# Attention and Fourier-mixing kernel: sequence table built on VectorE from the channel table's indices, the last keys of the first group turned apart, and a new order of instructions

## The chip, the cores and the metric

The kernel runs on one core of one Trainium2 chip. The metric is the device time of one execution in microseconds. The engines have short names in the profile: PE is TensorE (PEld its weight loads), DVE VectorE, ACT ScalarE, POOL GpSimd, SP SyncE. L12 is line 12 of the kernel.

## The reference

Attention with squared relus over 8 batches, 12 heads, 448 positions and 64 dimensions per head; then a block that adds the real part of a Fourier transform over positions and channels, normalises, and applies two dense layers.

```python
scores = matmul(q, k.transpose(0, 1, 3, 2)) / sqrt(64)
attn   = matmul(maximum(scores, 0.0) ** 2 / 448, v)
x      = attn.transpose(0, 2, 1, 3).reshape(8, 448, 768)
u      = x + real(fft(fft(x, axis=1), axis=2))
un     = (u - mean(u)) / sqrt(var(u) + 1e-06)          # over the 768 channels
out    = u + maximum(un @ w_ch1, 0.0) @ w_ch2          # 768 -> 3072 -> 768
```

## The kernel before

**How the order is made.** The kernel is written as some two dozen Python generators ("streams"): loads, tables, turning of q and k, attention, mixing, dense layers, stores. Each `yield need(engine, ...)` stands for one step, and the code behind it issues the instructions of that step. `Streams.run` takes one character after another from the string `ORDER`; a character is the index of the stream whose next step comes next. Streams that are finished drop out of the numbering, and new ones are added at its end. Every engine runs its instructions in the order in which they were issued, so the string fixes each engine's order. The times in `need` and in the class are the planner's; they steer a few choices (which bank, which engine), which `CHOICES` can overrule by their running number. The first streams are 0 `loading`, 1 `build_dft`, 2 `turning`, 3 `ffns`, 4 `mixes`, 5 `first_attention`, 6 and 7 `first_channels`, 8 `attentions`, 9 `warming`.

**The head (batch 0).** GpSimd issues the loads: q, k and v of a group of four heads, the last quarter of the keys and values as two separate half loads per tensor for all three groups (`load_halves`). Meanwhile `warming` (L2202) lets TensorE multiply zeros: the first step issues two products of 512 columns, each later one a product of 252 columns (L2216); it goes on until the first channel product. VectorE builds three tables of cosines and sines for the channel transform (`build_dft`, L364): for each table a rounded product (L372), its remainder (L374) and its absolute value (L376); ScalarE takes the sines (L381), and `negative` makes a negated copy (L441). The positions' table (`seq_table`, L401, and `seq_sines`, L418) is begun on GpSimd (two iotas, a scaling, two products, L406 to L414) and ended on VectorE (L421, L423, L425) and ScalarE (L431).

q and k of a group are turned by TensorE with eight transposes each for each of two pairs of heads (`turn_on_pe`, L654, r = 0 and 1), and one copy per pair brings the result to `qkT` (L678). Batch 0 has 21 score items (seven for each group). Item i is two products (L1002), a relu on ScalarE (L1017), and a square on VectorE (L1034); the last one is squared on ScalarE (L1031). Items 0 to 2 of a group need pair 0, item 3 the last keys of both pairs, items 4 to 6 pair 1. Six blocks of values (L870, L875) follow; each block is moved out in two halves (`fold`, L719 on ScalarE or L721 on VectorE), folded on VectorE (L796), and multiplied with the channel tables (L1457). The last block is moved by ScalarE, the two before it by the engine that the planner finds sooner free, the others by VectorE. The products of the two halves of the rows leave through two copies on ScalarE and two on VectorE (L1501).

**The end of the head** (`first_tail`, L1057). Four sets of rows t = 0 to 3, each in two halves: products with the positions' table (L1079, L1082), statistics (L1102, L1109), a root on ScalarE (L1115), a scaling on VectorE (L1122), a copy of the rows (L1131), the norm (L1152 on GpSimd for t = 0, 1, 2; L1154 and L1157 for t = 3), then a turn by TensorE (L1180) and its unloading (L1196, L1200) into the input of the dense layers. Of set 1 only 63 columns are turned there; a second turn for its other 64 follows later (`turn_rows`, L1255, L1260). There are three banks of the pool BS and two of BF for all this. Before the first root, ScalarE loads the table for roots (`root_table`, L448).

**The body** begins with batch 1's first score (stream `attentions`). From there attention of batches 1 to 7 is interleaved with the dense layers (L1986, L2015, L2126, L1817), which run on as one stream on TensorE.

Of the kernel before, what the change touches and what calls it, by code (L numbers as in the profile page):

```python
# [10 lines left out]
FP32 = mybir.dt.float32  # L11
# [30 lines left out]
class Banks(Bufs):  # L42
# [30 lines left out]
CODES = '0123456789ABCDEFGHIJKLMNOPQRSTUVWXYZ'  # L73
ORDER = "".join((
    '009000000200999999999999999991111N1N029919999909199G102NN10991F111888MM4400F11L88L88884L088M84L1',
    'ML480N1LM14LL0NM040LN1LLL41O0081M14LONL4L1ON401O410LQ88LLM41Q1041MMCKKNM300KP00737KQMKKNN3LP3N0L',
    'P7O30000LQ7PLLN3N0RPJJ73JLP6LPOIIJJJJL0634ML343JLJ4LL066JKKKK666KKJJJ343I03H2229G222GHG90GGG0GGG',
    'GGGGG00GGGGGGGGGGG0GGGHGGGGGG0GGHIGGGGGGGGGHIIGGGGGGGG7GHG213GFGGGF33FFHGFGF07F17EHE0GF3E1F1FF10',
    'F0F003GE000GG3FF01H1I30E0IFE1EGGEGE3HEHH3GG1GH1I1JI303III1I1KJI189ADFFBHGF1F3HFGG3FF1031JHH1HF3J',
    'G00IGH30GG1GGF31H1IHGF31F3HFGG30F1FF31G3F1GF3GF1FF3F3133C1022212H1F0E88FGF10FGI00G1HF11HNEEI11E8',  # L80
    'JJ0L00990011IHN0IHLKG555HHIAA10IHHF1HJG1HJJ1GJGJ555GGHH100GF3II1I1H1H55EHJEHG1GG2E3GG1GEDBFBD11H',
    '1I1IH31H3JJ5555555EG5555555E0GHHGEG1I555J3100EE0HE1H3KI0001CD77E9BKKIFEEHHGIIGG1GFKI31J871J3LLIE',
    'EIFFJDJEII101NILKI33PPFIDDKOOINNK000000DNOKOFLKMEN3L3OOIGKFNDFMFLIL0MM3JMM33NNIDD000DKH7G7000KHJ',
    'GJLJJLJ3LLHJLLGFF1GHDKI3H03KFDGIIGG000GDCFCD1FG2GG32212G3KG000JJII1IJGJ1JGJ3GD1J3PJN0KGOOJNL99N1',
    '1LSJNJPDDKJJ1QPRP301RJH1QJHOOLD7JJ1HQJJGL1ONI0NGM3UOCAQTTSMSQNSMKIKMMQNRMMKPMQLMRGJM63OQHJQQPML0',
    '000KKN66LKDOH0KLONJJ367F763MMIMGIKLDD33M000D000MMIKH11KKK88KK3HNJ1CAAGHFHC1GGGIGG1FGGDF2GF32212D',
    '3JFIIHHDD1HI1JI3F1JIF1FIFK3OKINNJMM1OIIF1POJIG1OM1NGN31ABBB8KK0000000NJGIG3VNIUNUTT1WIII1XTI1VVI',
    'IU31UIIFLJ3TRSSRR1TDMPPLMDLF1URD01TTS3SSS1000D1V1VS1UPTMT31T69CHH000G3SSSJQ1Q1RDHHKJR310111RDD7G',
    'GMIII3Q000DB000QQGPIIO1EOPPGRQOGDEGENJIM6OP0OQP3PHHGQQO788KK7OOLGMON3LEK663OMOKOEMKMGELDDH33NI00',
# [134 lines left out]
def kernel(  # L224
# [139 lines left out]
    def build_dft():  # L364
# [32 lines left out]

        for m in range(3):
            yield from channel_table(m)

    def seq_table():  # L401

        f = work.tile([128, 4 * KH], FP32, name="dfty", tag="uA", bufs=1)
# [1873 lines left out]
```

## Time and profile before

| | |
|---|---|
| median of 3 runs | 564.45 us (564.25 to 564.74) |
| the profiled execution's own time | 564.12 us |
| its span in the profile | 562.1 us |
| busy share of PE, DVE, ACT, POOL | 99%, 76%, 59%, 30% |

The span is the profile's time axis; the execution's own time has some 2 us more around it. A row of the timeline gives the start, the length, the engine, the line and the operation, the tiles (written first, then read), their shapes, and behind x how many instructions are merged; in square brackets stands the idle time in front and what ended it. Fillers count as busy time.

### The profile page before, as it was taken

The page shows a single profiled execution, that of the slowest core. Times are in us where ns is not written, and L with a number is a line of the kernel's source. Part 1 is how long each engine was busy: PE and PEld are TensorE (multiplying, and loading weights), DVE is VectorE, ACT ScalarE, POOL GpSimd, SP SyncE. Part 2 cuts the span into 40 slices and gives each one's busy share as a digit, 9 for nine tenths or more (in the row PEclk, how much of TensorE's full clock was granted, in tenths as well). Part 3 has the DMA queues.
Part 4 walks back from the last instruction along what each step waited for, and adds up shares of the span by engine and source line. Part 5 has one row for each costly group of instructions (what it writes and reads, how often), then busy time and mean ns, then how long its engine had stood idle before and what let it go on. Part 6 is the DMA issues. An engine that isn't in the chain of part 4 may idle for free.

```text
span 562.1 us, 11345 instructions
## 1 busy us (share of the span) xinstructions
PE 555.1 (99%) x4306; PEld 363.7 (65%) x4306; DVE 427.1 (76%) x1035; ACT 330.2 (59%) x557; POOL 166.8 (30%) x255
## 2 busy tenths in 40 slices
PE   8999999999999999999999999999999999999997
PEld 4376456576467554556756756856768688668864
DVE  7976576889787888887898788787898648544762
ACT  5977772777769678765686776657517054015400
POOL 8966224443334514434423243111011100000000
PEclk9999999999999999999999999999999999999999
DMA  9999999999999997999799989952445502314013
GB/s 111 180 206 266 204 208 147 183 172 172 147 120 222 146 195 144 142 239 184 124 153 183 214 165 166 207 139 64 114 117 159 162 30 47 96 42 141 1 43 114
DMA packets 152692, 82.46 MB, mean 147 GB/s; under 512 B 118077, under 2 KB 147901, under 8 KB 152637
## 3 DMA queue, kind: packets, MB, share of 16 engines
q0 software_dynamic: 57056, 33.63, 42.2%
q1 hardware_dynamic: 95580, 48.09, 39.9%
q8 instruction: 34, 0.56, 0.4%
q14 instruction: 22, 0.17, 0.1%
HBM read 62.91 MB, written 26.25 MB: 159 GB/s over the span
## 4 chain that ended last, share of the span: by engine, by line
PE 95%; DVE 1%; DMA 1%; ACT 1%; issue 0%; POOL 0%; DVEq 0%; POOLq 0%
PE psF L1986 27%; PE psF L2126 22%; PE psS L1002 8%; PE psS L2126 7%; PE psS L1817 7%; PE psF L875 5%; PE psF L2015 4%; PE psS L1482 2%; PE psF L1817 2%; PE psF L2040 1%; PE psF L870 1%; DMA kn<-in_k_dram 1%; PE psS L875 1%; PE psF L671 1%; PE psS L1457 1%; PE psS L1290 1%
## 5 line engine op out<-in xcount | busy, mean ns | idle before, releaser
L1017 ACT ACTIVATE sq<-psS 128x896 bf16<-128x896 f32 x168 | 145.9, 918 | 39.5 <-PE psS L1002 39.2
L1986 PE MATMUL psF<-unT,w 128*128 128x256 bf16 (+1 forms) x1296 | 165.6, 285 | 0.0
L1986 PEld LDWEIGHTS <-w 128*128 128x128 bf16 x1296 | 124.9, 98 | 38.0 <-issue 5.8
L2126 PEld LDWEIGHTS <-hT 128*128 128x128 bf16 x720 | 69.8, 98 | 47.0 <-issue 2.1
L1034 DVE TENSOR_TENSOR sq<-sq 128x896 bf16<-128x896 bf16 x138 | 82.5, 620 | 10.5 <-ACT sq L1017 9.9
L1973 ACT ACTIVATE hT<-psF 128x512 bf16<-128x512 f32 (+3 forms) x132 | 63.6, 503 | 41.3 <-PE psF L1986 40.8
L2126 PE MATMUL psF<-w,hT 128*128 128x384 bf16 x336 | 59.4, 326 | 0.0
L1674 DVE TENSOR_TENSOR o<-psF,o 128x384 f32<-128x384 f32 x73 | 40.4, 553 | 22.2 <-PE psF L2126 16.7
L1002 PE MATMUL psS<-qkT 64*128 64x448 bf16 (+1 forms) x336 | 51.8, 355 | 1.0 <-DVE qkT L678 0.9
L1832 ACT COPY copies<-psS 128x256 f32<-128x256 f32 x51 | 17.7, 376 | 53.5 <-PE psS L1817 40.2
L1391 POOL DMA_INDIRECT ubot<-u,backs x15 | 16.0, 1064 | 75.9 <-DVE u L1327 46.7
L1002 PEld LDWEIGHTS <-qkT 64*128 64x128 bf16 (+1 forms) x336 | 12.9, 94 | 32.7 <-issue 26.9
L524 POOL DMA_DIRECT2D qn<-in_q_dram x21 | 15.4, 735 | 61.7 <-DVE qkr L631 47.2
L875 PE MATMUL psF<-sq,vn 128*64 128x448 bf16 x234 | 31.5, 363 | 0.0
L1817 PEld LDWEIGHTS <-w 128*128 128x128 bf16 x288 | 28.2, 98 | 4.4 <-issue 0.7
L1334 DVE BATCH_NORM_STATS2 stats<-u 112x6 f32<-112x384 f32 (+2 forms) x56 | 29.8, 550 | 1.5 <-POOL u L1325 1.3
L737 DVE TENSOR_SCALAR xT<-psF 128x224 bf16<-128x224 f32 x56 | 19.8, 386 | 14.4 <-PE psF L875 14.1
L1391 POOL DMA_INDIRECT nbot<-un,backs x12 | 14.3, 1190 | 52.9 <-ACT un L1353 51.7
L1353 ACT ACTIVATE un<-u,small 112x768 bf16<-112x768 f32 (+2 forms) x28 | 28.7, 1029 | 1.3 <-DVE small L1340 0.9
L524 POOL DMA_DIRECT2D kn<-in_k_dram x21 | 16.1, 768 | 44.8 <-DVE qkr L631 37.8
L499 POOL DMA_DIRECT2D kn<-in_k_dram x42 | 25.8, 623 | 9.8 <-PE psF L1986 7.9
L1031 ACT ACTIVATE sq<-sq 128x896 bf16<-128x896 bf16 x30 | 28.3, 950 | 0.4
(245 smaller groups left out, 926.1 us busy)
## 6 DMA issues: line engine op xcount, KB each, us to landing
out_dram<-o SPq DMA_DIRECT2D x55, 192.0 KB, 3.5
qn<-in_q_dram POOLq DMA_DIRECT2D x21, 224.0 KB, 5.5
vn<-in_v_dram POOLq DMA_DIRECT2D x24, 192.0 KB, 6.5
w<-in_moe_w_ch_dram POOLq DMA_DIRECT2D x12, 384.0 KB, 10.7
w<-in_moe_w_ch_dram POOLq DMA_DIRECT2D x4, 1152.0 KB, 21.2
kn<-in_k_dram POOLq DMA_DIRECT2D x21, 192.0 KB, 5.8
utop<-u SPq DMA_DIRECT2D x12, 336.0 KB, 4.2
o<-utop SPq DMA_DIRECT2D x16, 192.0 KB, 2.6
```

The source lines that it names most:

```text
L524: nc.gpsimd.dma_start(out=to, in_=src[b, hs, 0:rows].rearrange("h (p j) d -> p h (j d)", j=j))
L875: nc.tensor.matmul(av[h * Dh:(h + 1) * Dh, 0:S], lhsT=vn_home[:, at:at + Dh], rhs=sq[:, h, :], start=start, stop=stop, skip_group_check=True)
L1002: nc.tensor.matmul(sc[:, h, 0:S].rearrange("k (c q) -> k c q", c=4), lhsT=flat[ps, k0:k0 + KB], rhs=qT[ps, pair], start=True, stop=True)
L1017: nc.scalar.activation(r, sc[:, :, 0:S], AF.Relu)
L1034: nc.vector.tensor_tensor(r, r, r, op=ALU.mult)
L1334: nc.vector.bn_stats(stats[:n, hf, :], u[:n, hf * (D // 2):(hf + 1) * (D // 2)])
L1391: nc.gpsimd.indirect_dma_start(out=bot, out_offset=bass.IndirectOffsetOnAxis(ap=(back if b < PAR else back2)[ch][:n], axis=0), in_=get(us[ ...
L1674: nc.vector.tensor_tensor(o[:, cols], pc[:, cols], o[:, cols], op=ALU.add)
L1817: nc.tensor.matmul(ps[:, 0:N], lhsT=lhs, rhs=rhs[:, m], start=(start and m == 0), stop=(stop and m == 2), skip_group_check=True)
L1973: nc.scalar.activation(hs, ps, AF.Relu)
L1986: nc.tensor.matmul(ph[:, i * N:(i + 1) * N], lhsT=w1_sb[m][hf][:, (jj + i) * 128:(jj + i + 1) * 128], rhs=unT[:, m, 0:N], start=(m == 0), ...
L2126: nc.tensor.matmul(pc[:, cols], lhsT=lhs[i], rhs=rhs[i][:, cols], start=(start and i == 0), stop=(i == KP - 1), skip_group_check=True)
```

## The change

1. **Sequence table.** GpSimd's part goes. The row indices are scaled copies of the channel table's, the column indices are read from its `dcol2` (0, 1, 2, ... stored as evens and odds, so read with a stride). For each of the two halves of 240 columns VectorE makes a rounded product and its remainder, then one absolute value of 480. The table is built behind the three channel tables in `build_dft`; its sines are taken when they were.
2. **Absolute value** in the channel tables by clearing the sign bit.
3. **Loads.** The iotas are issued behind the first q load, ahead of the first k load. The value halves go ahead of v of group 1.
4. **Last keys apart.** In group 0 the two pairs are turned with three of the four key quarters; four more transposes and one copy of 256 columns bring the last quarter of both pairs. Item 3 waits for it, items 0 to 2 and 4 to 6 do not.
5. **The last square** of batch 0 goes to VectorE.
6. **`root_table`** no longer names the first copies; the third norm is made by ScalarE in two halves; set 1 is turned once with 127 columns, and its second 64 are copied out at the end (`second_part`), until when its bank is kept.
7. **A new `ORDER`** (2,930 characters instead of 2,935) and new `CHOICES`.

The head's order, read character by character from the two strings (T q, T k: transposes of a pair; F: filler steps; s: score; sq: square; v: value; the number behind is the item; b: block; n: negation; c: copy of a turned pair):

```
PE, before:  F17 | T q r0 | F10 | T k r0 | F2 | T q r1, T k r1 | F3 | s0 s1 | F6 | s2 | F3 | s3 | T q | s4 | F1 | ...
             with 20 filler steps between s1 and the last values
PE, after:   F39 | T q r0 | F8 | T k r0 (six) | T q r1, T k r1 (six) | T last keys | s0 s1 s2 s3 | T q | v b0 | s4 | ...
             with 1 filler step between s1 and the last values
DVE, before: tables 0 1, n0, table 2, n1, c r0, n2, c r1, sq 0 1 2 3, ... sq 18, fold b0, sq 19, fold b1 b2,
             round, subtract, absolute (positions), fold b3 b4 b5, copies out
DVE, after:  tables 0 1 2, c r0, round, n0, c r1, n1, c last keys, subtract, n2, round, sq 0 1 2, subtract, sq 3, ...
             sq 16, (move b3), sq 17, fold b2 (half), b0, b1, absolute, fold b2 (half), b3, (move b4),
             sq 19, sq 18, sq 20, fold b4, fold b5, copies out
ACT, before: ... relu 20, move b4, sq 20, move b5, three sines, copies out, copy of batch 1's first pair, root table,
             rows t = 0, root 0, rows, ... root 3, unload 0, norm 3, unload 2, unload 3, rows 3
ACT, after:  ... relu 20, two sines, move b5, third sine, copies out, root table, rows 0, root 0, rows 0, rows 1,
             copy of batch 1's first pair, root 1, rows 1, rows 2, root 2, rows 2, norm 2 (two halves), root 3,
             unload 0, norm 3, unload 2, unload 3, rows 3
PE, channel products, before: the last three blocks' behind five fillers, one after another
PE, channel products, after:  b0 to b3, 16 transposes of batch 1, values of items 18 19 20, rest of b3, b4, F4, b5
```

(Brackets: a step that runs on VectorE or ScalarE, as the planner's times choose.)

```diff
-CODES = '0123456789ABCDEFGHIJKLMNOPQRSTUVWXYZ'
+CODES = '0123456789ABCDEFGHIJKLMNOPQRSTUVWXY'
 ORDER = "".join((
-    '009000000200999999999999999991111N1N029919999909199G102NN10991F111888MM4400F11L88L88884L088M84L1',
...
+    '0009000002009999999999199999999991999919999991N1N999999919092119999NN99919002121G220NN2G255212N5',
...
 CHOICES = {
...
     def build_dft():
...
-            nc.vector.scalar_tensor_tensor(g, f, -1.0, f, op0=ALU.mult, op1=ALU.max)
+            nc.vector.tensor_scalar(g.bitcast(mybir.dt.int32), f.bitcast(mybir.dt.int32), 0x7FFFFFFF, None,
+                                    op0=ALU.bitwise_and)
...
+        nc.vector.tensor_scalar(row[:, 0:2], row[:, 4:6], 1.0 / S, None, op0=ALU.mult)
         nc.vector.tensor_scalar(row[:, 4:7], row[:, 4:7], 1.0 / D, None, op0=ALU.mult)
...
+        if SEQ_AT == 3:
+            yield from seq_table()
     def seq_table():
...
+        cols = dcol2.rearrange("p (t k) -> p k t", t=2)[:, 0:SX // 2]
         for i in range(2):
...
+            yield need("DVE", dve(SX))
+            nc.vector.tensor_scalar(wi, cols, drow[:, i:i + 1], None, op0=ALU.mult)
+            yield need("DVE", dve(SX))
+            nc.vector.scalar_tensor_tensor(fi, cols, drow[:, i:i + 1], wi, op0=ALU.mult, op1=ALU.subtract)
+        e = yield need("DVE", 0.4)
+        nc.vector.tensor_scalar(whole, f.bitcast(mybir.dt.int32), 0x7FFFFFFF, None, op0=ALU.bitwise_and)
+        sch.add(seq_sines(f, g, e), (0, SEQ_RANK))
...
     def root_table():
-        yield need("SP", 0.0, [dft_ready, last_relu, first_copied])
-        yield need("ACT", 1.5, [first_copied])
+        yield need("SP", 0.0, [dft_ready, last_relu])
+        yield need("ACT", 1.5, [dft_ready])
...
-            if i == 0 and x == 1:
+            if i == 0 and x == 0:
                 e = yield need("POOL", 0.55)
                 dft_indices()
...
     def loading():
-        for i in range(NG):
-            yield from load_group(i)
+        yield from load_group(0, (0, 1), (0,))
+        yield from load_halves(0, 0, NG, 1)
+        yield from load_group(0, (2,), (0,))
+        yield from load_group(1, (0, 1), (0,))
+        yield from load_halves(0, 0, NG, 2)
+        yield from load_group(1, (2,), (0,))
+        yield from load_group(2)
...
-        yield from seq_table()
...
     def turn_on_pe(b, g):
...
+        first = i == 0
+        w = 4 * R + (3 if first else 4) * KB
...
-                for c in range(4):
+                for c in range(3 if first and x else 4):
...
-            copy(pairs[:, r], pt[:, 0:4 * (KB + R)])
+            copy(pairs[:, r, 0:w], pt[:, 0:w])
...
+        if first:
+            e1 = yield need("PE", 4 * 0.07, ready[i][1:2], [BF])
...
+                    nc.tensor.transpose(pt[h * Dh:(h + 1) * Dh, r], loads[i][1][:, 3, 2 * r + h, :], ident)
+            e2 = yield need("DVE", 0.28, [e1 + LATENCY["PE"]])
+            nc.vector.tensor_copy(pairs[:, :, w:], pt)
...
-            sch.add(square(b, r, e + LATENCY["ACT"], sqs[i][1], b == 0 and i == NB - 1), (0.2, 0.2))
+            sch.add(square(b, r, e + LATENCY["ACT"], sqs[i][1]), (0.2, 0.2))
...
         def turn(t, k):
             n, idn, c0, w = turned_cols(t)
+            if t == 1:
+                idn, w = rev[:, 0:127], 127
...
         def unload(t, en, part=None):
...
-                BS.give(pts[t][0], last)
+                if t != 1:
+                    BS.give(pts[t][0], last)
...
+        def second_part():
+            e = yield need("DVE", dve(6 * 64), [done[1][0]])
+            nc.vector.tensor_copy(groups[1][2][:, :, 0:64].rearrange("p (h m) w -> p h m w", h=2),
+                                  pts[1][0][:, :, 0:384].rearrange("p h (m w) -> p h m w", w=128)[:, :, :, 63:127])
+            BS.give(pts[1][0], e)
...
-        yield from norm(2, 0, "POOL")
+        yield from norm(2, 0, "ACT")
+        yield from norm(2, 1, "ACT")
...
-        sch.add(turn_rows(uns[0][1], max(t_un[1]), 128, rev[:, 63:127], 0, 64, "DVE", second_un[0]), (1, 1))
+        sch.add(second_part(), (1, 1))
```

117 lines of the change are left out of this document (58 added, 59 removed), and 38 rows, old and new, of the table CHOICES.

## The prediction

> **What bounds the kernel now.** I read the page first (its span, and the chain of waits by engine), then busy time by stage, then the timeline of the head, and last the groups of VectorE.
>
> ```profile
> span 562.1 us, 11345 instructions
> PE 95%; DVE 1%; DMA 1%; ACT 1%; issue 0%; POOL 0%; DVEq 0%; POOLq 0%
> ```
>
> The chain that ended last is 95% TensorE, but this average mixes a head, where fillers count as work, with a body. So the stages (columns: window, length, then busy time of PE, PEld, DVE, ACT, POOL):
>
> ```profile
> 10.40:28.50 18.10, 18.02 (x162) 7.57 (x161) 17.11 (x35) 18.00 (x24) 17.25 (x50) 1.00 1.32 175
> 34.60:45.60 11.00, 10.57 (x114) 8.18 (x111) 8.61 (x26) 8.16 (x18) 7.27 (x10) 1.00 1.08 222
> 45.60:558.70 513.10, 512.45 (x3906) 338.64 (x3906) 389.67 (x941) 294.68 (x500) 129.22 (x172) 1.00 0.80 145
> ```
>
> From 45.6 us to the last product TensorE is idle for 0.65 us of 513.10, and no filler is in it. The products there are the same after the change. So the body can hardly be shortened by taking waits out of it, only lengthened, and what the change can win is the moment at which the body begins: 45.6 now. In 10.40:28.50 (batch 0's scores) TensorE, ScalarE and VectorE are all nearly full; VectorE has 0.99 us free. The head's start and end, in the timeline:
>
> ```profile
> 1.27 4.09 PE L2216 MATMUL psS<-warm 128*128 128x512 bf16 x18 [1.27 <-DVE warm L319]
> 2.18 0.82 POOL L524 DMA_DIRECT2D qk<-in_k_dram  x1
> 3.19 0.52 POOL L312 IOTA dcol<- 128x386 f32 x1
> 3.30 0.59 DVE L385 TENSOR_SCALAR drow<-drow 128x3 f32<-128x3 f32 x1 [0.98 <-POOL drow L310]
> 4.00 0.44 DVE L372 TENSOR_SCALAR dftr<-dcol,drow 128x386 int32<-128x386 f32 x1
> 5.12 0.56 DVE L376 SCALAR_TENSOR_TENSOR dfty<-dfty 128x386 f32<-128x386 f32 x1
> 5.32 0.39 PE L671 MATMUL psF<-ident,qk 112*64 112x112 bf16 x8
> 5.64 1.25 PE L2216 MATMUL psS<-warm 128*128 128x252 bf16 x10
> 7.59 0.24 PE L671 MATMUL psF<-ident,qk 128*64 128x128 bf16 x1 [0.30 <-DMA qk<-in_k_dram]
> 9.31 0.65 DVE L678 COPY qkT<-psF 128x960 bf16<-128x960 bf16 x1
> 10.43 11.83 ACT L1017 ACTIVATE sq<-psS 128x896 bf16<-128x896 f32 x14
> 27.89 0.61 DVE L1034 TENSOR_TENSOR sq<-sq 128x896 bf16<-128x896 bf16 x1
> 28.79 1.01 ACT L1031 ACTIVATE sq<-sq 128x896 bf16<-128x896 bf16 x1
> 30.75 0.38 PE L875 MATMUL psF<-sq,vn 128*64 128x448 bf16 x2
> 31.18 0.61 ACT L719 ACTIVATE xT<-psF 128x224 bf16<-128x224 f32 x2 [1.38 <-PE psF L875]
> 33.50 1.05 ACT L1501 CAST pc<-psS 128x386 bf16<-128x386 f32 x2
> 34.72 0.96 ACT L678 COPY qkT<-psF 128x960 bf16<-128x960 bf16 x1 [0.16 <-PE psF L671]
> 35.68 1.28 ACT L448 ACT_TABLE_LOAD   x1
> 37.18 0.46 ACT L1131 COPY u<-psS 128x384 f32<-128x384 f32 x1
> 42.87 0.29 ACT L1115 ACTIVATE small<-small,few 112x1 f32<-112x1 f32 x1 [0.99 <-DVE small L1109]
> 43.75 0.67 ACT L1154 ACTIVATE un<-psF,small 112x384 bf16<-112x384 f32 x1
> 44.56 0.64 ACT L1196 CAST unT<-psS 128x576 bf16<-128x576 f32 x1
> 45.10 0.41 ACT L1200 CAST unT<-psS 128x291 bf16<-128x291 f32 x1
> 45.63 0.36 PE L1002 MATMUL psS<-qkT 64*128 64x448 bf16 x2
> ```
>
> The first turned keys are copied only at 9.31, although their last transpose (7.59) is long done: VectorE is still building tables. The relus (11.83 over 14, 0.845 us each) then run unbroken. At the end the last square (28.79) lets the last values go at 30.75, and on ScalarE a copy and the table load stand between 34.72 and the first rows out, 37.18. The row of 45.63 is the body's first product.
>
> **The change, part by part.** Each engine's order is the one listed above from the new ORDER string.
>
> *Start.* The iotas go ahead of the keys' load, so the indices come 0.82 us sooner (the 2.18 row); the keys land up to 0.7 later (the iotas' time, 0.52 and a little), which TensorE's fillers hide. The tiny scaling doubles: its second costs between 0.1 and 0.59 us (the 3.30 row); I take 0.1, because the long one ran beside an iota. The tables then begin near 3.3 instead of 4.00. From 4.00 to the copy at 9.31 are three tables and two negations, so a table takes 1.6 us; with the absolute value as a bit operation 0.2 less (0.56 against the 0.41 of L425 below). Three tables end near 7.5.
>
> But the copy of the keys, next on VectorE, waits for TensorE, which now runs 48 filler products before the key transposes instead of 28. The first 18 hold it to about 5.1; later ones cost 0.108 us each (the chain's row of 31.59 below: 0.54 for five). So 22 more reach 7.5, eight transposes (0.32, from 5.32 to 5.64) and eight fillers 8.7, six transposes 8.95, and the copy starts near 9.2: 0.1 sooner than now, with 1.6 us that VectorE has gained standing idle. That this copy no longer waits for the last keys buys nothing, since they have landed by then. Were the fillers at full speed from 1.27 on, the copy would come at 7.6.
>
> The page "TensorE: Matmul & The Clock Gate" of the Trainium skill, section "What's actually happening", has the array at half its clock until one window of some 3.4 us was busy, with the window free-running. The first 18 fillers against the later ten agree with half a clock; had the gate opened 0.5 us later, the copy would come some 0.25 us later still.
>
> *VectorE through the scores.* Its groups between 9.3 and 31.5 us, a row of two moves, two pieces of the chain, and ScalarE's waits for statistics (total, times, longest):
>
> ```profile
> L1034 DVE TENSOR_TENSOR sq<-sq 128x896 bf16<-128x896 bf16 x20 | 11.9, 633 | 0.7 <-ACT sq L1017 0.6
> L678 DVE COPY qkT<-psF 128x960 bf16<-128x960 bf16 x6 | 3.9, 653 | 0.2 <-PE psF L671 0.2
> L796 DVE TENSOR_TENSOR fold<-xT 128x225 bf16<-128x225 bf16 x10 | 2.3, 287 | 0.0
> L423 DVE TENSOR_TENSOR dfty<-dfty 128x480 f32<-128x480 f32 x1 | 0.7, 659 | 0.0
> L441 DVE TENSOR_SCALAR channeg<-chan 128x386 bf16<-128x386 bf16 x2 | 0.5, 261 | 0.5 <-ACT chan L381 0.5
> L425 DVE TENSOR_SCALAR dfty<-dfty 128x480 int32<-128x480 int32 x1 | 0.4, 410 | 0.0
> L421 DVE TENSOR_SCALAR dfty<-dfty 128x480 int32<-128x480 f32 x1 | 0.4, 397 | 0.0
> 23.33 0.69 DVE L721 TENSOR_SCALAR xT<-psF 128x224 bf16<-128x224 f32 x2
> 31.59 0.54 PE psS L2216 x5
> 32.13 2.00 PE psS L1457 x24
> ACT small L1115 <- DVE small L1109: 2.6, 3, 1.0
> ```
>
> From the first copy (9.31) to the end of square 19 (28.50) VectorE now does 6 copies, 20 squares, 6 moves, one negation and two folds. The new order has in the same stretch, to the end of square 20, besides these: one square (0.6); the last keys' copy (0.25: 256 columns, between the 0.26 of L441 and the 0.65 of 960 columns) less what two shortened copies save (0.14); two negations that stood before it (0.4); the sequence table's first four operations at half length (two of 0.27, two of 0.42, together 1.4: half of L421 and L423 plus a fixed part; at the least 1.06, the bare halves, and at most 2.1, the full rows, since they read with a stride); its bit operation (0.36); and six folds at 0.2 (1.2). That is 4.05. Of the 1.4 us that VectorE idles there (0.99 in the window, and L441's wait of 0.5 ahead of it) I fill 1.1. So square 20 ends near 28.5 - 0.1 + 4.05 - 1.1 = 31.3; on ScalarE it is done at 29.80. What is late next are the last values: on TensorE they stand behind 16 transposes (0.6) and two values (0.3 each) and begin near 32.0, and the move of 31.18 comes at 32.25, 1.05 later. Had VectorE kept up, ScalarE's relus and moves would end this stage 1.65 us sooner than that.
>
> *Channel products.* Today 24 short products (0.083 each) come last and end at 34.13; in the new order only eight stand behind the last fold, and they end at 34.15: level. The copies out start on ScalarE at 34.05 instead of 33.50.
>
> *Table load and rows.* The copy of 34.72 (0.96) moves behind the first rows out, so the load begins at 35.1 and the first rows leave at 36.7, 0.5 sooner. The row products end within 0.3 us of today.
>
> *Norms.* ScalarE now has that 0.96 copy and the two halves of the third norm (0.64 each by the 43.75 row, less overlap) in this stretch, which GpSimd did; its 2.6 us of waits for statistics take them in, but not where they lie best. It is free today from 41.88 (42.87 less 0.99); the third scale is there about then, the halves end at 43.25, and the fourth root comes at 43.25 instead of 42.87, the move of 44.56 at 45.1. The second rows' bank is now kept until the second part is out, so half of the last turn waits for this move, to 45.75; the move of 45.10 comes at 46.05 and frees the bank of the body's first product at 46.45, today 45.6. The six products of the second turn that are dropped (they stood just ahead of it) are inside this difference. GpSimd's sequence operations cost nothing today, as it only feeds a queue of loads; were the body short of weights, taking them out would be a gain.
>
> Sum: 564.12 us of the profiled execution (the span 562.1 and 2.0 around it) + 0.85 = 564.97. The median of the runs, 564.45, lies 0.33 above that execution, so 565.3.
>
> **The rivals.** (a) VectorE does not end the scores: its operations overlap more than I add up, or the fillers cost less. Then the 1.65 us are had: 563.7, between 563.0 and 564.4. For it: its tables are done by 7.5. Against: the 48 fillers, and 17.11 busy of 18.10.
>
> (b) Slower: blocks 3 and 4 are moved by ScalarE now, but the planner's times choose the engine, and the diff does not show which. Each on VectorE puts 0.69 us ahead of square 20. One gives 566.0, both 566.7; it decides from the second on. Against: the rule that chose ScalarE is unchanged.
>
> (c) Slower: the new order puts holes into the full body. Half of the 0.43 us that 34.60:45.60 is idle, once in each of seven batches, adds 1.5: 566.8. For it: the body has no slack to take a hole in. Against: 0.65 idle in 513.10 under the old order.
>
> (d) Slower: with the fillers gone from the scores (20 now, one then) TensorE falls back to the rate of its first products. A stretch as long as the first (4.09) adds 2 us of products where the fillers leave 2.2 free, so it decides from the second stretch on: 567.2. Against: TensorE stays busy for most of this stage without them. The same page of the Trainium skill, section "A second HAM failure mode: psum-queue depth-cycling", has frequent small pauses between groups of products bring the gate down; no run here shows that.
>
> **How the numbers follow.** Own forecast 0.50 (564.3 to 566.3), (a) 0.20, (b) 0.16, (c) 0.09, (d) 0.05. A measurement of this kernel tells about 0.2%, 1.13 us: below 563.32 or above 565.58. Of the forecast's half, 0.34 lies within and 0.16 above; (a) gives 0.10 faster and 0.10 within; (b) 0.02 within and 0.14 slower; (c) and (d) are slower. Faster 0.10, same 0.46, slower 0.44. The range takes most of (a), the price of the strided operations, and (b) and (c): 563.2 to 567.0.
>
> **What would show it.** Right: the first key copy near 9.2 with VectorE idle ahead of it; VectorE full until past 31; the last square over a microsecond behind the last relu; first rows out before 37.2; the body's first product after 46, and the body about 513 us long. Wrong: a key copy at 8 or earlier, last values before 31, or a body more than 0.5 us longer or shorter, which I hold for fixed.

## The result, and the profile after

The changed kernel took 569.75 us (median of 5 runs, 568.06 to 571.18); the kernel before, on the same chip, 564.37 (564.25 to 564.74). The ratio is 1.0092 [1.0068, 1.0116]: 0.9% slower, and above the range forecast (563.2 to 567.0). The profiled execution took 571.18, 7.06 more than that of before, and is the slowest of the five. From the page, its span and the chain of waits:

```profile
span 569.3 us, 11342 instructions
PE 89%; DVE 4%; DMA 2%; SPq 2%; ACT 2%; issue 0%; DVEq 0%
```

TensorE's share of the chain fell from 95% to 89%. The stages of after (window, length, busy time of PE, PEld, DVE, ACT, POOL, then the granted clock):

```profile
10.16:13.58 3.42, 1.84 (x28) 0.92 (x22) 3.34 (x10) 2.06 (x3) 3.27 (x8) 1.00 1.53 147
13.58:16.99 3.41, 3.41 (x28) 1.21 (x26) 2.14 (x5) 2.49 (x4) 3.35 (x18) 0.50 1.43 168
47.20:565.90 518.70, 514.18 (x3908) 339.44 (x3906) 392.30 (x942) 295.12 (x501) 131.04 (x172) 1.00 0.82 144
197.90:201.30 3.40, 2.10 (x14) 1.10 (x13) 3.37 (x8) 1.43 (x2) 1.64 (x3) 1.00 1.51 186
272.99:276.40 3.41, 1.10 (x12) 0.80 (x9) 1.60 (x4) 1.41 (x2) 0.00 (x0) 1.00 1.18 317
276.40:279.81 3.41, 3.41 (x18) 2.39 (x16) 3.38 (x8) 1.30 (x2) 0.00 (x0) 0.50 1.02 261
```

The third row is the result. The body is 518.70 us long instead of 513.10. TensorE idles 4.52 us of it instead of 0.65, so 3.87 of the 5.60 are waits. The other 1.73 are busy time for the same products: in 276.40:279.81 the granted clock is 0.50, and 3.41 us at half clock do 1.7 us of work. The half clock isn't in every execution: the run at the median, 569.75, had a mean granted clock of 1.0, and so no such window. The waits themselves, TensorE's in the body of after (what was waited for, total, times, longest):

```profile
PE psF L2021 <- DVE xT L758: 2.3, 1, 2.3
PE psF L2021 <- DMA unT<-nbot: 1.3, 1, 1.3
PE psF L2161 <- DVE o L1709: 0.4, 1, 0.4
PE psF L2021 <- DVE hT L2006: 0.3, 1, 0.3
```

Before has a single one, of 0.3, at another product (L1817). The two long ones in the timeline of after; SPq is SyncE's queue, and L1465 and L865 are DMA transposes:

```profile
195.62 1.25 SPq L1465 DMA_TRANSPOSE unT<-nbot  x1
...
201.11 1.14 PE L2021 MATMUL psF<-unT,w 128*128 128x384 bf16 x6 [1.30 <-DMA unT<-nbot]
...
266.53 3.21 SPq L865 DMA_TRANSPOSE xn<-xT  x2
...
270.36 0.76 PE L898 MATMUL psF<-sq,vn 128*64 128x448 bf16 x6
274.77 0.69 DVE L758 TENSOR_SCALAR xT<-psF 128x224 bf16<-128x224 f32 x2 [4.51 <-DMA xn<-xT]
275.51 1.93 PE L2021 MATMUL psF<-unT,w 128*128 128x256 bf16 x12 [2.31 <-DVE xT L758]
```

And the same instructions in the timeline of before:

```profile
188.37 1.23 SPq L1430 DMA_TRANSPOSE unT<-nbot  x1
...
198.29 3.09 PE L1986 MATMUL psF<-unT,w 128*128 128x384 bf16 x18
...
249.15 2.58 SPq L844 DMA_TRANSPOSE xn<-xT  x2
...
267.47 0.69 DVE L737 TENSOR_SCALAR xT<-psF 128x224 bf16<-128x224 f32 x2 [0.66 <-PE psF L875]
```

At 201 TensorE wants the turned second half of a dense input. Its transposition was issued at 195.62, 4.2 us before TensorE went idle (201.11 less 1.30 is 199.81); in before it had 9.9 us (188.37 to 198.29). At 275 VectorE may overwrite `xT` with a block of batch 5 only when batch 4's third tile has been transposed out of it. That transposition stands on SyncE behind others and was issued 3.7 us before VectorE had nothing else to do (274.77 less 4.51 is 270.26, less 266.53), 4.6 before the values to be moved were there (270.36 and 0.76); in before it was some 18 us ahead. VectorE stood 4.51 us, and TensorE behind it 2.31. So from issue to use the first transposition took 5.5 us (195.62 to 201.11) and the second 8.2 (266.53 to 274.77). For comparison the medians from issue to landing of the two kinds, of before and then of after (DMA issues: times, median us):

```profile
xn<-xT SPq DMA_TRANSPOSE x42, 5.1
unT<-nbot SPq DMA_TRANSPOSE x10, 2.7
```

```profile
xn<-xT SPq DMA_TRANSPOSE x42, 4.9
unT<-nbot SPq DMA_TRANSPOSE x10, 4.9
```

Both took longer than the median of their kind in either kernel.

The head of after, in the timeline:

```profile
1.27 7.35 PE L2251 MATMUL psS<-warm 128*128 128x512 bf16 x40 [1.27 <-DVE warm L319]
7.64 0.36 DVE L378 TENSOR_SCALAR early<-early 128x386 int32<-128x386 int32 x1
8.55 0.39 PE L680 MATMUL psF<-ident,qk 112*64 112x112 bf16 x8
10.24 0.59 DVE L687 COPY qkT<-psF 128x832 bf16<-128x832 bf16 x1 [2.23 <-PE psF L680]
15.38 0.92 ACT L1040 ACTIVATE sq<-psS 128x896 bf16<-128x896 f32 x1 [0.46 <-PE psS L1025]
29.74 0.68 ACT L740 ACTIVATE xT<-psF 128x224 bf16<-128x224 f32 x2
30.73 1.68 DVE L1057 TENSOR_TENSOR sq<-sq 128x896 bf16<-128x896 bf16 x3
32.42 0.73 PE L898 MATMUL psF<-sq,vn 128*64 128x448 bf16 x6
36.16 1.28 ACT L448 ACT_TABLE_LOAD   x1
46.27 0.64 ACT L1223 CAST unT<-psS 128x576 bf16<-128x576 f32 x1 [0.60 <-PE psS L1205]
47.27 0.37 PE L1025 MATMUL psS<-qkT 64*128 64x448 bf16 x2
```

The body begins at 47.27 instead of 45.63, 1.64 later. Of the execution's 7.06, 1.64 come from the head and some 5.5 from the body.

### The profile page after: what moved, and what is told of

It reads as the page before. It is cut to its first block, busy times and chain, and to the rows that moved or that the text cites. A ratio compares the mean times of both kernels' runs of the same rounds, so it can differ in the third digit from the quotient of the medians.

```text
span 569.3 us, 11342 instructions
## 1 busy us (share of the span) xinstructions
PE 556.5 (98%) x4295; PEld 365.1 (64%) x4295; DVE 429.2 (75%) x1040; ACT 330.9 (58%) x558; POOL 164.6 (29%) x249
## 4 chain that ended last, share of the span: by engine, by line
PE 89%; DVE 4%; DMA 2%; SPq 2%; ACT 2%; issue 0%; DVEq 0%
PE psF L2021 27%; PE psF L2161 19%; PE psS L2161 7%; PE psS L1852 7%; PE psS L1025 7%; PE psF L898 4%; PE psF L2050 4%; PE psF L1852 3%; PE psS L1517 2%; PE psS L2251 2%; DMA xn<-xT 1%; DVE sq L1057 1%; PE psF L2075 1%; PE psF L893 1%; SPq L1465 1%; DMA unT<-nbot 1%
## 5 line engine op out<-in xcount | busy, mean ns | idle before, releaser
L2021 PE MATMUL psF<-unT,w 128*128 128x256 bf16 (+1 forms) x1296 | 167.3, 286 | 3.9 <-DVE xT L758 2.3
L1426 POOL DMA_INDIRECT ubot<-u,backs x15 | 19.0, 1264 | 52.3 <-DVE u L1362 47.1
L898 PE MATMUL psF<-sq,vn 128*64 128x448 bf16 x234 | 31.3, 366 | 0.2 <-DVE sq L1057 0.2
L1426 POOL DMA_INDIRECT nbot<-un,backs x12 | 12.7, 1056 | 61.7 <-ACT un L1388 42.5
L526 POOL DMA_DIRECT2D vn<-in_v_dram x24 | 18.8, 782 | 38.9 <-PE psS L1025 38.0
L501 POOL DMA_DIRECT2D kn<-in_k_dram x42 | 25.8, 623 | 12.3 <-PE psF L2021 7.2
L1872 DVE CUSTOM_DVE_ANT_0 hT<-psS,copies 128x256 bf16<-128x256 f32 x40 | 15.9, 418 | 16.5 <-ACT copies L1867 9.6
## 6 DMA issues: line engine op xcount, KB each, us to landing
w<-in_moe_w_ch_dram POOLq DMA_DIRECT2D x12, 384.0 KB, 11.5
```

Source lines behind the costliest of these rows:

```text
L526: nc.gpsimd.dma_start(out=to, in_=src[b, hs, 0:rows].rearrange("h (p j) d -> p h (j d)", j=j))
L898: nc.tensor.matmul(av[h * Dh:(h + 1) * Dh, 0:S], lhsT=vn_home[:, at:at + Dh], rhs=sq[:, h, :], start=start, stop=stop, skip_group_check=True)
L1426: nc.gpsimd.indirect_dma_start(out=bot, out_offset=bass.IndirectOffsetOnAxis(ap=(back if b < PAR else back2)[ch][:n], axis=0), in_=get(us[ ...
L2021: nc.tensor.matmul(ph[:, i * N:(i + 1) * N], lhsT=w1_sb[m][hf][:, (jj + i) * 128:(jj + i + 1) * 128], rhs=unT[:, m, 0:N], start=(m == 0), ...
```

## The experiments

Each was timed beside the kernel before on its own chip (564.34 to 564.63). The expectations name theories by letters: A, the body's new order costs the time; B, the head does; the others stand for what is said beside them. Edits of the order are given as the engine's list, as in the change.

**Head and body apart.** The first kernel has the changed head, up to batch 1's first score, and from there the old order and choices; the second is the reverse.

```diff
-ORDER = new head + new body
+ORDER = new head + old body        # first
+ORDER = old head + new body        # second
```

> The changed kernel's head, step for step up to batch 1's first score, and behind it the steps of the body in the order and with the bank and engine choices of the kernel before. The changed kernel's profile has its body's first product at 47.27 us (45.63 before) and a body of 518.6 us (513.1 before), with TensorE waiting 2.31 us at 275.5 and 1.30 at 201.1. Theory A (the holes belong to the new body's order: its transposes by DMA and its dense products stand too close): the body is 513 us again, no wait of TensorE over 0.5 us in it, total 564.4 + 1.6 = 566.0 (565.5 to 566.5), runs within 0.5 us of one another. Theory B (the holes come from the head: it ends later, so loads and transposes are shifted against the products whatever the order): the body keeps holes of 3 to 5 us and the total stays between 568 and 571.

> The reverse: the head of the kernel before, step for step up to batch 1's first score, and the body's steps in the changed kernel's order with its choices. Theory A (order of the body): first product of the body at 45.6 as before, a body of 516 to 519 us, total 567 to 570, with a spread over the runs of more than 1 us. Theory B (late head): no holes over 0.5 us, total 564.4 plus or minus 0.5.

The new head alone: 565.77 us (565.24 to 566.74, 10 runs), 1.0022 [1.0013, 1.0031]. The new body alone: 570.23 (568.07 to 574.86, 6 runs), 1.0109 [1.0077, 1.0141], with waits of 2.5 and 1.4 us at the two places shown above. With the old body under the new head, the stage row is

```profile
47.20:560.60 513.40, 512.40 (x3907) 338.80 (x3906) 389.85 (x943) 294.66 (x500) 129.37 (x172) 1.00 0.81 145
```

513.40 us, 0.30 over before. Theory A holds, B falls: the body's order costs about 4 us behind the new head (569.75 less 565.77) and 5.7 behind the old one (570.23 less 564.51), the head about 1.3. Taken alone, body and head cost together 7.0, more than the whole change (5.4).

**Which transpositions.** Both late ones are put earlier on SyncE in the changed kernel; then only the one of batch 4.

```diff
 SyncE, batch 4:  ... nbot, q/k, xn second tile
+                 xn third and fourth tile
                  q/k, ntop, ntop, out, nbot, out
-                 xn third and fourth tile
 SyncE, batch 3:  ntop
-                 xn third tile              # only in the first of the two
                  nbot
+                 xn third tile              # only in the first of the two
```

> The changed kernel, with SyncE's queue mended at the two places where TensorE stood in its profile. The transposition of batch 4's third channel tile (and the fourth) is issued ahead of the stores and of the dense input's transpositions that stood before it (in the kernel before, too, it comes ahead of them), and at batch 3 the first transposition of a channel tile goes behind the dense input's second half instead of ahead of it. Nothing else is moved. Theory A1 (these two issues make the holes): the 2.31 us at 275.5 and the stretch of clock 0.50 behind it go, the 1.30 at 201.1 shrinks to 0.3 or less; body 513.5 to 515, total 565.8 to 567. Rival (the holes come from the crowded DMA rings or from VectorE's order, and move on): total 568 or more, with other waits of TensorE over 1 us.

> As the run before, with the first place alone (batch 4's third and fourth channel tiles). Theory A1: the wait of 2.31 us goes and the one of 1.30 stays; the total is about 1 to 1.5 us above that run's, 567 to 568.5. Rival: no gain against the changed kernel, 569 or more.

Both mended: 567.01 (564.18 to 569.4, 6 runs), 1.0053 [1.0039, 1.0067], an interval below that of the whole change. One mended: 566.19 (565.29 to 571.77, 12 runs), 1.0037 [1.0019, 1.0055]: no different from both. In the profiled execution of the first (564.18 us) TensorE's waits in the body are

```profile
PE psF L2257 <- DVE o L1805: 0.4, 1, 0.4
PE psF L2117 <- DVE hT L2102: 0.3, 1, 0.3
```

and its stages

```profile
44.90:558.90 514.00, 512.77 (x3908) 338.81 (x3906) 393.05 (x943) 295.22 (x501) 131.76 (x172) 1.00 0.81 146
10.16:13.58 3.42, 2.16 (x22) 0.90 (x19) 3.42 (x10) 3.18 (x4) 3.24 (x8) 1.00 1.60 155
```

The distances are 5.7 us at the first place (192.18 to 197.84) and some 20 at the second: no wait, no half clock, a body of 514.00. The edit moves these issues and nothing else, so these waits came from the distance between issue and use. At the second place no profile of a kernel with the mend has a wait of TensorE. But the profiled execution is the fastest of the six; the median stays some 2.5 us above before, and the runs differ by 5 us: something else is left. And since one mend does as well as two, what the place at 201 costs the median isn't shown. The kernel with one mend showed in a profiled execution of 571.25 us a wait of 1.1 at 201, which it leaves unmended, and one of 2.2 us near 103, for an addition of VectorE to the dense layers' output `o`, that the changed kernel's own trace doesn't have.

**Where in the body.** New head; the new order up to batch 3 (about 149 us) and the old one behind; the reverse; and a later cut.

```diff
-ORDER = new head + new body
+ORDER = new head + new body to 149 us + old body           # first
+ORDER = new head + old body to 149 us + new body           # second
+ORDER = new head + new body to batch 5 + old body          # third
```

> The changed kernel with its own head and its own order up to batch 3's first score (about 149 us), and from there the old order with its choices. Theory H (the loss lies where transpositions are issued close to their use, at 201 and 275): both places have the old distances, no wait of TensorE over 0.6 us behind 150; total 565.5 to 567 (the head's 1 to 2 us, and now and then a wait near 100). Rival (the loss is spread, or lies in the first 100 us of the body): 567.5 or more.

> The reverse: the changed kernel's head, the old order up to batch 3's first score, the new order behind it. Theory H: the waits near 201 and 275 are back, total 568 to 571, spread over 2 us. Rival: under 567.

> As the first of these, cut at batch 5's first score (about 245 us), so that the place near 201 is in and the one near 275 is not. Theory H: a wait of 0.5 to 2 us near 201 in most executions, none near 275; total 566.5 to 568.5, between the other two. Rival (the wait near 275 is a late consequence of the first): 565.5 to 566.5 or as much as the second.

First: 565.62 (563.95 to 569.28, 14 runs), 1.0015 [1.0007, 1.0024], level with the new head on the old body. Second: 569.89 (568.54 to 570.03, 5 runs), 1.0091 [1.0077, 1.0104], the whole loss of the change. Third: 571.53 (570.97 to 572.1, 4 runs), 1.0129 [1.0114, 1.0143]; its cut came at about 296 us, behind the last moves of batch 5, and not near 245 as its text has it, so it holds both places, and its wait of 1.4 at 276 says nothing against the theory. The second kernel's waits:

```profile
PE psF L2117 <- DVE xT L854: 2.6, 1, 2.6
PE psF L989 <- DMA vn<-in_v_dram: 1.5, 1, 1.5
PE psF L2117 <- DMA unT<-nbot: 1.3, 1, 1.3
```

The one for `vn`, batch 1's values, lies at 54 in the old order; the other two are at the known places, and this execution (570.03 us) has no half clock in its body. Waits alone can make the loss.

The first kernel's profiled execution was its slowest (569.28), with one wait, near 103, and a half clock at 104.3:

```profile
PE psF L2146 <- DVE o L1805: 3.0, 1, 3.0
```

So from batch 3 on the loss is steady, and ahead of it there is a place near 102 that costs 3 to 4 us in some executions, in this kernel too few to move the median.

**The old order with late transposes.** The same two tiles late in the kernel before:

```diff
 SyncE, batch 4:  ... xn second tile
-                 xn third and fourth tile
                  ntop, q/k, q/k, out
+                 xn third and fourth tile
```

> The kernel before, untouched but for one thing: on SyncE's queue the transpositions of batch 4's third and fourth channel tiles are issued behind the output store that follows them much later, so at about 265 instead of 249.2 and 250.5. The move into the same tile for batch 5 comes at 267.5 there. In the changed kernel the distance is 3.8 us (266.5 against 270.3) and TensorE stands for 2.3 us. Theory A1 (this distance alone makes the hole): VectorE waits 1 to 5 us for the transposition at 267.5, TensorE 0.5 to 3.5 us behind it, perhaps with a stretch of clock 0.50 after it; total 565.2 to 568.5. Rival (the hole needs the rest of the new order): total 564.2 to 564.8.

564.41 (564.23 to 565.86, 11 runs), 1.0000 [0.9990, 1.0009]. The test was weaker than meant: SyncE was free, so they were issued at 257.7, still some 10 us ahead of the move. The first of the two landed 7.4 us behind its issue. So some 10 us are enough there, and 3.7 would not have been; what that would have cost was not measured.

**VectorE slowed by GpSimd.** In the trace of after one addition takes 2.64 us where its like take 0.55, just while GpSimd does two additions (VectorE, then GpSimd):

```profile
179.97 0.55 DVE L1360 TENSOR_TENSOR u<-qs,xn 112x385 f32<-112x385 f32 x1
180.44 2.64 DVE L1362 TENSOR_TENSOR u<-tp,xn 112x383 f32<-112x383 f32 x1
...
180.92 0.93 POOL L1360 TENSOR_TENSOR u<-tp,xn 112x385 f32<-112x385 f32 x1
181.80 0.85 POOL L1362 TENSOR_TENSOR u<-qs,xn 112x383 f32<-112x383 f32 x1
```

The page "SBUF — State Buffer" of the Trainium skill, section "🔬 SBUF: two separate sides", has VectorE's operations with two inputs in SBUF and GpSimd's share a port pair that only one holds at a time, for a whole instruction. The 2.64 against 0.55 agrees: VectorE's addition ends at 183.08, behind both of GpSimd's. That it waited although it began 0.48 us before the first of them is left unexplained.

Is this the cause of the lateness? Theory G: yes. Three kernels do these additions on VectorE: one with all the mends of the last experiment below (two transpositions, fillers, iotas); the changed kernel without a mend; and one with the two transpositions mended.

```diff
-            eng, en, d = ((nc.vector, "DVE", 2 * dve(KN)), (nc.gpsimd, "POOL", 1.8))[i and not (b > 2)]
+            eng, en, d = nc.vector, "DVE", 2 * dve(KN)
```

> All mends of the run before (head with 17 first fillers, fillers in the scores, iotas behind k; both transpositions mended), and the additions of the second half of the rows of batches 1 and 2 on VectorE instead of GpSimd, at the same places of the order. Theory G (VectorE's additions are held up by GpSimd's, and what stands behind them on VectorE lets TensorE wait at about 101 and 201 us): no addition of VectorE over 0.8 us, no wait of TensorE over 0.6 us after 60 us, every execution between 563.9 and 565.2, median 564.0 to 564.6. Rival (the late loads behind these places are the cause, and VectorE gets 4.4 us more work): executions above 567 as before, or a median of 565 or more.

> The changed kernel, with the additions of batches 1 and 2 on VectorE as its only difference. Theory G: the wait of 1.30 us at 201.1 goes, the wait of 2.31 at 275.5 (batch 4's transposition) and the slow stretch behind it stay: total 566.5 to 569, 1 to 3 us under the changed kernel. Rival: no change, 569 to 571.

> The changed kernel with its own head, the body mended in all three ways (both transpositions, additions on VectorE). If the body's loss is the three places, the body is 511.5 to 513 us long and what is left is the head: two groups of executions, near 564.2 where the clock opens at about 4.5 us and near 566 where it opens at 6.5 or later and falls back in the scores; median 565 to 566. If something else in the new body costs time, 566.5 or more.

568.84 (565.7 to 571.66, 6 runs), 1.0057 [1.0036, 1.0078]; 572.33 (567.93 to 576.76, 6 runs), 1.0157 [1.0117, 1.0197]; 569.62 (566.4 to 573.94, 6 runs), 1.0095 [1.0062, 1.0129]. No addition took over 0.56 us any more. Yet the first is 4.0 us over its like without the edit (564.84, last experiment), with intervals apart, and the third 2.6 over the two mends, with intervals that just overlap. Of the second's six runs three took 567.9 to 570.0, like the whole change, and three 574.7 to 576.8. The first one's waits:

```profile
PE psF L2116 <- DMA unT<-nbot: 3.2, 1, 3.2
PE psF L2145 <- DVE o L1804: 2.1, 1, 2.1
```

The place at 201 and the one near 102 wait without a stretched addition too, so G is not shown. Nor is it ruled out for the changed kernel: the edit gives VectorE GpSimd's additions to do, where in after it is busy already for 22.26 of the 24 us from 180 on. The first wait above fits the distances again: in spite of the mend the transposition was issued at 196.93, 4.3 us before TensorE went idle (201.26), and TensorE went on at 204.49, 7.6 behind the issue.

**The head's fillers.** All with the old body: 15 fillers between the first scores; 17 first fillers instead of 39; the latter with batch 1's values loaded ahead of the second half of a weight; both kinds of filler edit, with and without that load.

```diff
 PE:  F39 | T q r0 | ... | s0 s1
+     F6
      s2
+     F3                        # and ahead of the next two scores
-PE:  F39 | T q r0
+PE:  F17 | T q r0              # few first fillers
 GpSimd, loads:
-     w1 second half, values of batch 1
+     values of batch 1, w1 second half
```

> As e1, with 15 more filler steps between batch 0's scores: six ahead of the third score, three each ahead of the fourth, fifth and sixth. In the changed kernel TensorE is busy for 1.84 of 3.42 us from 10.16 to 13.58, and the granted clock is 0.50 from 13.58 to 16.99; VectorE then waits 1.53 us for transposes at 17.25. Theory C (the missing fillers cost the clock, and the slow stretch delays the stage): no stretch of clock 0.5 behind the start, no wait of VectorE over 0.5 us between 10.3 and 32, the last square ends 1 to 1.5 us earlier than in e1 and the body begins 1 to 1.5 us earlier; total 564.5 to 565. Rival (the slow stretch lies beside ScalarE's and VectorE's own work, and fillers only take TensorE's time): body's first product within 0.3 us of e1's, total within 0.3 of e1.

> As e1, with 17 filler steps ahead of the first transposes instead of 39, as many as the kernel before has. In the changed kernel VectorE's tables end at 8.0 and the first turned keys are copied at 10.24, VectorE idle for 2.23 us ahead of it, waiting for TensorE. Theory D (the fillers hold the key transposes up): the copy starts at 8.1 to 8.8, the last square ends 1 to 2 us earlier than in e1, and the body begins 1 us or more earlier; total 564.5 to 565.2. Rival (the transposes wait for the keys' landing, or the fewer products open the clock later): copy after 9.5, body's first product within 0.4 of e1's, total within 0.4 of e1.

> The new head with 17 first fillers and the old order of the body, as in the run with fewer first fillers, and batch 1's values loaded ahead of the second half of the first dense weights instead of behind it. In that run the body began at 44.77, 0.86 us before that of the kernel before, but TensorE then waited 1.45 us at 54.40 for those values, and the median came to 565.64. Theory E (the head's gain is given back at batch 1's values, which lie behind six loads of weights): no wait for values, the last products start at about 44.8 + 511.2 = 556.0 (556.6 in the kernel before), total 563.5 to 564.2. Rival (the loads only change places and the weights come late instead, or TensorE's next wait takes over): total 565 or more.

> As the run before, with 15 filler steps more between batch 0's scores, as in the run that kept the clock up there. With fewer first fillers some executions have shown a mean clock of 0.990 to 0.997. Theory C2 (these come from slow stretches in the scores, which the fillers prevent): every execution at 0.999 or above, a smaller spread, median 0.1 to 0.4 us lower. Rival (the scores wait for loads and for ScalarE there, and fillers only delay them): median equal or up to 1 us higher.

> The new head with 17 first fillers and 15 fillers between the scores, the loads in the changed kernel's order, and the old body: the base of the next run. With the old body, batch 1's eighth relu (the row that I compare) starts at 60.62 in the kernel before and at 61.89 to 62.85 with the new head, whether the body's first product stands at 44.77 or at 47.83, and from there on the distance to the kernel before does not change any more. Theory F (the loads of batch 1 set this row, not the head's end): 61.5 to 62.5 again, median 565.3 to 565.9, no execution with a mean clock below 0.998. Rival (the head's end sets it): about 60 and 564.0.

In this order: 565.70 (564.9 to 566.73, 11), 565.64 (564.98 to 566.23, 11), 566.13 (564.93 to 568.22, 9), 565.82 (565.59 to 567.48, 7) and 566.28 us (565.58 to 567.28, 8); ratios 1.0020 [1.0012, 1.0029], 1.0019 [1.0010, 1.0028], 1.0032 [1.0020, 1.0044], 1.0027 [1.0016, 1.0038], 1.0031 [1.0020, 1.0042]. All are level with the new head unedited, and the gains expected were missed. The profiled executions (us; the clock is full from the trace's first record of a granted clock of 1.0):

| kernel | clock full from | first key copy | last square ends | body begins | last product |
|---|---|---|---|---|---|
| before | 4.92 | 9.31 | 29.80 | 45.63 | 558.49 |
| after | 6.75 | 10.24 | 32.41 | 47.27 | 565.63 |
| new head, old body | 6.67 | 10.20 | 32.38 | 47.24 | 560.29 |
| score fillers | 6.40 | 10.06 | 31.68 | 46.54 | 560.28 |
| few first fillers | 5.83 | 7.93 | 29.72 | 44.77 | 559.76 |
| few, values first | 4.71 | 7.94 | 32.97 | 47.83 | 560.72 |
| two mends (above) | 4.45 | 9.12 | 30.13 | 44.99 | 558.55 |

Few first fillers bring the body 0.86 us ahead of before, and the last product still comes 1.27 behind: TensorE then waits 1.4 us for batch 1's values (loaded from 37.4 on, in before from 36.4). With the values first there is no such wait, but the clock was at half for 10.24 us from 11.5 on; with score fillers too the clock stayed full, and TensorE waited for the next loads, q and k (1.1 and 0.7). So what the head wins is given back at batch 1's loads. The eighth relu of batch 1, in before and then in the new head on the old body:

```profile
60.62 2.54 ACT L1017 ACTIVATE sq<-psS 128x896 bf16<-128x896 f32 x3 [0.35 <-PE psS L1002]
```

```profile
62.42 0.92 ACT L1136 ACTIVATE sq<-psS 128x896 bf16<-128x896 f32 x1 [0.36 <-PE psS L1121]
```

It is 1.80 late there, and the last product is 1.80 late too: with the old body nothing is won or lost behind it. That score fillers keep every execution at full clock fell as well: with few and score fillers the runs at a granted clock of 1.0 took 565.6 to 565.9, those at 0.996 or 0.997 took 566.6 to 567.3.

**The iotas.** The last of these kernels with the iotas back behind the first k load:

```diff
-            if i == 0 and x == 0:      # iotas ahead of k
+            if i == 0 and x == 1:      # iotas behind k
```

> As the run before, with the channel table's iotas behind the first k load again, as in the kernel before, so that the chain of loads on GpSimd starts 0.64 us sooner (k at 2.18 instead of 2.83) and the tables up to 0.8 later. Theory F: the weights' and values' loads are issued 0.4 to 0.6 us sooner and the eighth relu of batch 1 starts 0.4 to 0.6 us sooner than in the run before, the median 0.3 to 0.6 lower. Rival (the tables and the head's end matter more): the row and the median stay or rise by up to 0.8.

565.13 (565.06 to 565.65, 11 runs), 1.0010 [1.0001, 1.0019]: 1.15 under its like (566.28), with the eighth relu 0.49 sooner in the profile (61.79 for 62.28) and no run below a clock of 0.999. So the whole row of loads, delayed by the iotas, is worth 0.5 to 1.1 us; how much of it is the clock these runs don't tell apart.

**All mends.** The changed kernel with both transpositions mended, 17 first fillers, 15 score fillers and the iotas behind k:

> All mends in one: the changed kernel's head with 17 first fillers, 15 fillers between the scores and the iotas behind the first k load, and the changed kernel's body with the transpositions of both places mended. If the two holes of SyncE's queue and the head's clock are the whole loss: 564 to 565.5, level with the kernel before. If the new body has further places that stand too close to its loads and transposes, as the two executions near 571.5 of the run with one mended place suggest: 565.5 to 568, with a spread over 2 us.

564.84 (564.13 to 569.67, 11 runs), 1.0013 [0.9995, 1.0032]: level with the kernel before. Three of its runs took 566.8 to 569.7. One of these was profiled:

```profile
PE psF L2145 <- DVE o L1804: 2.4, 1, 2.4
```

The place near 102 again. No version was faster than the kernel before.

## Why the prediction was wrong

**The step that failed** is the one that holds the body at 513 us: "The products there are the same after the change. So the body can hardly be shortened [...], only lengthened". It was lengthened, by 5.6 us in the profiled execution. Rival (c) named it, holes from the new order, and priced it at half of a head's idle time seven times over, 1.5 us, with 0.09. The holes are not small pauses in every batch but two distances. The order of both kernels was at hand: in the old one batch 4's third and fourth tiles are transposed ahead of batch 5's first block, in the new one behind it. Their length shows in the trace of after alone: 3.7 to 4.6 us, which falls short of the 5.1 that the median of its kind was in before, and 4.2 us, which doesn't fall short of 2.7; its transposition took 5.5 us here. What is more, in the profiled execution one such wait was followed by a window at half clock, 1.7 us on top of 2.3; the prediction had a falling clock (rival d) for the head only.

**The head** was forecast at 0.85 later and measured 1.26 with the old body behind it (ratio interval: 0.7 to 1.8), 1.64 in the profiled execution. Its steps:

- First key copy 9.2: it came at 10.24, with VectorE idle ahead of it for 2.23 us, as described (the tables ended at 8.00, not 7.5, which this wait hid). The clock became full at 6.75 and not near 5.1. In the execution in which it did at 4.45, the copy came at 9.12. That is 1.12 for 2.30 us of clock, the forecast's own 0.25 for each 0.5. The term was right, the moment was not.
- The last square at 31.3: it ended at 32.41. But with the early clock it ended at 30.13. VectorE was then busy for 20.81 of the 21.01 us from the first copy on, before for 17.77 of 19.19 up to square 19: 3.04 us more work and not 4.05. That is the part of rival (a) in which operations overlap; VectorE still ended the stage. In the profiled execution the square is 2.28 later, 1.12 from the first copy and 1.16 from the stage behind it, which holds the half clock of 13.58:16.99: rival (d), which the prediction let decide from a second slow stretch on. This first one already had a price, and the second came in the body.
- Behind the square the sum of the steps was right to 0.3: 14.86 us from its end to the body, forecast 15.15, before 15.83. Blocks 3 and 4 stayed on ScalarE (rival b did not happen).
- "The keys land up to 0.7 later [...], which TensorE's fillers hide": those keys yes, but every load behind them is later as well, and batch 1's first scores and values pay for it. That half of the move was not followed down GpSimd's queue.

Left open: what sets off the wait near 102, which came in some executions only. VectorE is late there behind a late load of keys (in the profile of the all-mends kernel it idles 2.94 for one until 94.48), and the wait came with the stretched addition (2.68 us there) and without it (the first of the kernels with the additions on VectorE, 3.56 of idling until 95.69). In the changed kernel's own trace VectorE idles 1.91 for that load, no addition there is stretched, and TensorE doesn't wait. No experiment took that load away.

## What to carry to other kernels

When an order is changed, list for each transfer how far its issue lies ahead of its first use, in both orders, and set it against the times from issue to landing that the trace shows, the long ones rather than the median (here 5.5 to 8.2 us where the medians were 2.7 to 5.1); do so too for buffers that a transfer must leave before they are overwritten. "The same products" says nothing about waits where the bounding engine is full. And a gain at the head is worth nothing until the loads that the next stage waits for come sooner too.

## What the runs showed of the hardware

A wait could cost more than its length: the 3.41 us from 272.99, with TensorE busy 1.10 (32%), were followed by 3.41 us at half clock, as were those from 10.16 with 1.84 of 3.42 (54%); 2.10 of 3.40 (62%) at 197.90 were not. The Trainium skill, "TensorE: Matmul & The Clock Gate", section "What's actually happening", puts the fall behind an idle window of about 3.4 us; the length agrees, but here a window half busy could be enough. The busy share alone does not decide: windows with 1.69 of 3.41 (few and score fillers, 51.29), 1.77 of 3.42 (new order from batch 3 on, 271.38) and 1.86 of 3.41 (new body alone, 273.84) were followed by full clock.

The clock of one and the same head became full at moments from 4.45 to 6.75 us in different executions, with fillers from 1.27 on in all of them, and each such microsecond moved the first key copy by half of one (9.12 to 10.24).

A DMA transposition that an engine waited for took 5.5 and 7.6 us (a dense input) and 8.2 (a tile of `xT`) from issue to use, where the medians to landing were 2.7 to 5.1. Another tile of `xT` landed 7.4 us behind its issue with nothing waiting for it.
